# Spectral filter and gated MLP on one core: fifteen pairs of block products, denser dealing, low parts by GpSimd's queue, three twiddle copies

## The chip, the cores and the metric

One core of a Trainium2 chip runs the whole kernel. The metric is device time in microseconds (us). Before the change three runs took 1389.22, 1392.01 and 1394.37 us; the median is 1392.01. PE is the matrix engine, DVE the vector engine, ACT the scalar engine, POOL is GpSimd, SP the engine that here only issues DMAs. A DMA is issued by SP or by GpSimd, each in the order of its own instructions.

## The reference

```python
def reference(A_x, A_w_r, A_w_i, B_x, B_w_gate, B_w_up, B_w_down, gate_w):
    x = A_x                                            # 1 x 2048 x 576
    g = sigmoid((x * gate_w).sum(-1, keepdims=True))
    X = rfft2(x, axes=(-2, -1)) * (A_w_r + 1j * A_w_i)
    a = irfft2(X, s=(2048, 576), axes=(-2, -1))        # spectral branch
    h = gelu(B_x @ B_w_gate) * (B_x @ B_w_up)          # 576 -> 4608
    b = h @ B_w_down                                   # 4608 -> 576
    return g * a + (1 - g) * b
```

In this kernel the MLP reads the same x. All is float32.

## The kernel before

**The MLP is PE's work.** A float32 operand is split into a high part (rounded for the fast matmul) and a low part (the rest); a product takes three matmuls: high by high, low by high, high by low. The 4608 hidden features are 36 weight blocks of 128, taken in 18 pairs. Tokens are taken in two halves of 1024 (p = 0, 1), each as two column blocks of 512 (tb = 0, 1). One step n of the main loop is one pair of weight blocks for one tb: four chains (line 756, `chain`) of 14 matmuls of 512 columns, gate and up for each of two weight blocks, and, for the step before, four `down` (line 836) that multiply by the down weights (48 matmuls of 288 columns). Results go to a staging tile `stg` (four buffers) and from there into `yd` in DRAM, by a DMA on GpSimd's queue that adds to what is there; the first of each is a plain store on SP.

**Products.** For p = 1 the last pairs are done otherwise (`products`, line 1023): the two column blocks of tokens and two parts of the features form a 2 by 2 block product, done as seven products of sums (Strassen's way, in Winograd's form), each seven matmuls for gate and for up (`seven`, line 1009), with the sums of weights made by DVE (`prep_b`, line 985) and the sums of outputs added up by DVE (line 1051). That is 98 matmuls of 512 columns for a pair, where the ordinary way takes 112. The pairs from `FIRST` on go this way: i = 4 to 17 before. The operands are sums of x that are made once (`operands`, `last_operand`).

**Low parts in DRAM.** Weight blocks are needed twice, for p = 0 and p = 1. The low part of a weight block is a subtraction by DVE. For the first 2 x `FIRST` weight blocks, which p = 1 takes the ordinary way, `lower` (line 730) stores the low part in DRAM (`lo`) when p = 0 makes it, and p = 1 loads it instead of making it: 640 KB for the gate and up weights (into `gu`, three buffers) and 288 KB for the down weights (into `dn`, four buffers). Before, these loads are issued by SP, among the loads of raw weights (`raws<-wgu`, `raws<-wd`) and of x for the second half (`xraw<-xt`, line 1177, through four small buffers that ACT and DVE empty).

**The spectral branch runs beside it, mostly on DVE and ACT.** It is a generator that yields its costs: row transforms of the two halves (`forward_rows`), a column stage (`columns`) with its own matmuls on PE (line 274), and the way back (`last_tiles`, `inverse_rows` for h = 0 and 1). The matmuls of the MLP earn credit, `RATE` us for each us of PE time (`tick`, line 645); the MLP's own DVE work is taken from the credit. At each `gap` (line 653; twelve in a step n) the generator is run while there is credit, and stops early where it yields None. So `RATE` sets how much DVE work is queued per us of PE time, and so in which step each part of the branch stands. In the column stage a second generator (`beside`, line 293) does work on other tiles with what credit is left. `at(n, fn)` puts an instruction n gaps later. The results of the branch are added to `yd` by GpSimd: from `til` for h = 0 (line 607), from `xraw` and `cns` for h = 1 (line 597).

**Twiddles** multiply a complex tile by a constant rotation: ACT makes a scaled copy, DVE combines it with the tile (`_twiddles`, line 104 on). Whole tiles are turned by `tile_twiddles` (line 414), with two temporary tiles in the column stage and four in `last_tiles`.

**Operands** of the products are made in `operands`, woven into the last inverse transform by `woven` (line 562): at each second step of the main generator before.

Of the kernel before, what the change touches and what calls it, by code (L numbers as in the profile page):

```python
# [26 lines left out]
SW = 2 * (KF + 1)  # L27
ROWS = 5120
UNIT = ROWS // 4
RATE = 1.04  # L30
STEP = 6
FIRST = 4
ROW_BLOCK = (0, 6, 3, 5, 8, 1, 2, 7, 4)


# [68 lines left out]
def _twiddles(eng, act, unit, real, imag, places, tmps, sgn, cost):  # L104

    todo = list(places)
    ahead = min(2, len(tmps) - 1)

    def scaled(i):
        if i < len(todo):  # L110
            at, n = todo[i]
            s = 1.0 if n == 4 else sgn * math.sin(math.pi * n / 8)
            act.activation(tmps[i % len(tmps)][0], unit(*at), AF.Copy, scale=s)

    yield None
    for i in range(ahead):
        scaled(i)
    yield None
    for i, (at, n) in enumerate(todo):
        scaled(i + ahead)  # L120
        c, (_, tr, ti) = math.cos(math.pi * n / 8), tmps[i % len(tmps)]
        xr, xi = real(*at), imag(*at)
        if n == 4:
            act.activation(xr, ti, AF.Copy, scale=-float(sgn))
            act.activation(xi, tr, AF.Copy, scale=float(sgn))
            continue
        eng.scalar_tensor_tensor(xr, xr, c, ti, op0=ALU.mult, op1=ALU.subtract)
        yield cost
        eng.scalar_tensor_tensor(xi, xi, c, tr, op0=ALU.mult, op1=ALU.add)
        yield cost  # L130


def _block_of_token():
# [25 lines left out]
def _build(nc, tc, a):  # L159
    with ExitStack() as ctx:  # L160
# [8 lines left out]
        def f(x):  # L169
            return x.bitcast(F32)  # L170
# [59 lines left out]
        def columns():  # L230
# [62 lines left out]
            def beside():  # L293

                more = gates()
                tmps = [flat[:, SW * i:SW * (i + 1)] for i in (1, 2)]
                for d in range(1, 4):
                    yield from tile_twiddles(d, TAKEN, -1, tmps)
                    yield from four(d, TAKEN, sp, -1)
                    made[0] = d  # L300
                for d in range(3):
                    while gone[0] < (4 * d + 5) * STEP + 5:
                        yield next(more, None)
                    yield from four(d, range(4), sp, 1)
                yield from more
                for k in (1, 2):
                    yield from tile_twiddles(k, LEFT, 1, tmps)
# [19 lines left out]
            for kb in range(18):  # L327
# [18 lines left out]
                for g in range(STEP):  # L346
                    if g == 0:
                        while kb % 4 == 2 and kb < 14 and made[0] < kb // 4 + 1:
                            credit[0] -= next(side[0])
                        if on:  # L350
                            v = product(0, kb, xh, xl)
                            load_ww(kb + 1)
# [60 lines left out]

        def tile_twiddles(k, at, sgn, tmps):

            tmps = [(x, x[:, 0:NK], x[:, NK:]) for x in tmps]
            places = [((k, at[o]), o * k) for o in range(1, 4)]
            yield from _twiddles(vec, act, lambda d, e: T[:, d, e], lambda d, e: T[:, d, e, re],
                                 lambda d, e: T[:, d, e, im], places, tmps, sgn, 0.5)

        def last_tiles():

            rows = rows_tile()
            sp = rows[:, 0:4 * SW].rearrange("p (e k) -> p e k", e=4)
            yield from tile_twiddles(3, LEFT, 1, [rows[:, SW * i:SW * (i + 1)] for i in range(4, 8)])
            yield None
            yield from _butterfly(vec, lambda i: T[:, i], lambda i: T[:, i, :, re], lambda i: T[:, i, :, im],
                                  range(4), sp, 1, (2.6, 1.35))
# [132 lines left out]

        def woven(main, other):

            n, free = 0, 0
            for v in main:
                yield v
                n += 1
                if n % 2 == 0 and reloaded[0] and count[0] > free:
                    w = next(other, 0.0)
                    if w is None:  # L570
                        free = count[0]
# [158 lines left out]
        def lower(key, g, r, cost):  # L730
            j, i = key[1], key[0] == "dn"
            if NT <= j < NT + 2 * FIRST:
                nc.sync.dma_start(f(g[:, 1]), lows[j - NT][i])
                return

            def run():
# [574 lines left out]
```

## Time and profile before

| what | value |
|---|---|
| median of three runs | 1392.01 us |
| the profiled execution | 1387.69 us |
| its span (first to last instruction) | 1385.8 us |
| mean granted PE clock | 0.998 |
| matmuls | 7490 |

The page of the profile gives busy time by engine, and the span in 40 slices of 34.6 us. A digit is the busy share in tenths, 9 standing for 90% and more:

```profile
PE   9999999999999999999998999999999999999998
DVE  6989999998877876999979873587777777777776
ACT  5553434355656665444464549445555555555552
POOL 0021111121222211111141023212111121111110
DMA  9577765668899996556789588767667667776776
```

The stages lie so in time: p = 0 with the row transforms to about 320 us, the column stage to about 540, the way back to about 820; p = 1 begins in slice 21, and products run from 884 us to the end. A matmul's shown end is modelled and overlaps the next, so PE reads as busy through short waits; where it loses time is seen better from the windows and from the list of waits, where the engine that waited stands first and what released it second.

### The profile page before, as it was taken

What the parts mean: (1) busy time and instruction counts of PE and PEld (TensorE: products, weight loads), DVE (VectorE), ACT (ScalarE), POOL (GpSimd) and SP (SyncE); (2) the same over time, 40 slices, a digit from 0 to 9 for tenths busy, and PEclk for the clock granted to TensorE, in tenths of its full rate; (3) what the DMA queues carried; (4) which work ended last, traced back from release to release, by engine and by line L of the source; (5) the groups of instructions that cost most, each with busy time, mean ns of one, the idle gap of its engine ahead of it and who ended that gap; (6) DMA issues with size and microseconds to landing.
All of it is one profiled execution on the core that took longest, in us unless ns stands there. A gap on an engine that the chain in (4) does not pass through costs nothing.

```text
span 1385.8 us, 20125 instructions
## 1 busy us (share of the span) xinstructions
PE 1366.2 (99%) x7490; PEld 1206.0 (87%) x7490; DVE 1119.8 (81%) x1649; ACT 703.8 (51%) x1095; POOL 266.2 (19%) x326
## 2 busy tenths in 40 slices
PE   9999999999999999999998999999999999999998
PEld 7888888888888888888887888888888888888887
DVE  6989999998877876999979873587777777777776
ACT  5553434355656665444464549445555555555552
POOL 0021111121222211111141023212111121111110
PEclk9999999999999999999999999999999999999999
DMA  9577765668899996556789588767667667776776
GB/s 341 198 179 153 180 116 97 123 117 185 213 272 260 247 235 121 99 112 124 148 185 253 197 171 189 141 128 131 130 129 130 130 130 131 127 129 130 131 154 172
DMA packets 102226, 226.65 MB, mean 164 GB/s; under 512 B 12400, under 2 KB 22640, under 8 KB 101744
## 3 DMA queue, kind: packets, MB, share of 16 engines
q0 software_dynamic: 45248, 92.56, 44.0%
q1 hardware_dynamic: 56880, 132.81, 30.2%
q8 instruction: 59, 0.97, 0.3%
q14 instruction: 39, 0.32, 0.1%
HBM read 118.56 MB, written 99.61 MB: 157 GB/s over the span
## 4 chain that ended last, share of the span: by engine, by line
PE 58%; DMA 1%; DVE 1%; ACT 0%; issue 0%; SPq 0%; DVEq 0%; ACTq 0%
PE pdn L821 20%; PE pgu L1016 4%; PE pgu L1018 4%; PE pgu L1017 4%; PE px L1016 3%; PE px L1018 3%; PE px L1017 3%; PE pgu L762 2%; PE pgu L763 2%; PE pgu L761 2%; PE px L761 2%; PE px L763 2%; PE px L762 2%; PE pgu L1019 2%; PE px L1019 1%; DMA gu<-lo 1%
## 5 line engine op out<-in xcount | busy, mean ns | idle before, releaser
L834 POOL DMA_DIRECT2D yd<-stg x264 | 230.1, 872 | 1028.3 <-ACT stg L846 975.3
L846 ACT ACTIVATE stg<-pdn,omg 128x576 f32<-128x576 f32 x272 | 201.9, 742 | 380.2 <-PE pdn L821 282.1
L821 PEld LDWEIGHTS pdn<-dn,hb 128*128 128x128 f32 x2760 | 382.0, 188 | 11.6 <-DVE raws L875 0.5
L821 PE MATMUL pdn<-dn,hb 128*128 128x288 f32 x2760 | 389.9, 295 | 0.2 <-DVE raws L875 0.2
L762 PE MATMUL pgu<-xhi,gu 128*128 128x512 f32 x440 | 172.5, 392 | 4.2 <-DMA gu<-lo 3.9
L761 PE MATMUL pgu<-xhi,gu 128*128 128x512 f32 x440 | 172.6, 392 | 1.1 <-ACT gl L799 1.1
L763 PE MATMUL pgu<-xlo,gu 128*128 128x512 f32 x440 | 172.1, 391 | 0.0
L213 ACT ACTIVATE gu<-raws 128x1280 fp32r<-128x1280 f32 (+3 forms) x84 | 86.4, 1029 | 38.8 <-PE px L767 28.3
L762 PEld LDWEIGHTS pgu<-xhi,gu 128*128 128x128 f32 x440 | 82.9, 189 | 19.7 <-DMA gu<-lo 4.4
L761 PE MATMUL px<-xhi,gu 128*128 128x512 f32 x256 | 100.0, 390 | 0.0
L763 PE MATMUL px<-xlo,gu 128*128 128x512 f32 x256 | 99.8, 390 | 0.0
L762 PE MATMUL px<-xhi,gu 128*128 128x512 f32 x256 | 99.7, 389 | 0.0
L763 PEld LDWEIGHTS pgu<-xlo,gu 128*128 128x128 f32 x440 | 83.0, 189 | 18.1
L761 PEld LDWEIGHTS pgu<-xhi,gu 128*128 128x128 f32 x440 | 83.0, 189 | 16.3 <-ACT gl L799 1.5
L821 PEld LDWEIGHTS pdn<-dn,gu 128*128 128x128 f32 x672 | 92.2, 188 | 2.1
L821 PE MATMUL pdn<-dn,gu 128*128 128x288 f32 x672 | 93.5, 295 | 0.0
L807 DVE TENSOR_TENSOR hb<-gl,hb 128x512 fp32r<-128x512 f32 x88 | 60.4, 687 | 38.0 <-ACT hb L213 37.9
L799 ACT ACTIVATE gl<-pgu 128x512 f32<-128x512 f32 x55 | 32.8, 596 | 92.3 <-PE pgu L768 85.8
L1034 DVE TENSOR_TENSOR xraw<-xraw 128x512 f32<-128x512 f32 x56 | 38.8, 693 | 31.2 <-ACT xraw L1042 30.7
L1051 DVE TENSOR_TENSOR gl<-gl,pgu 128x512 f32<-128x512 f32 x56 | 38.3, 684 | 27.8 <-PE pgu L1019 27.8
L763 PEld LDWEIGHTS px<-xlo,gu 128*128 128x128 f32 x256 | 48.1, 188 | 10.4
L213 ACT ACTIVATE hb<-gl 128x512 fp32r<-128x512 f32 x88 | 54.9, 624 | 3.3 <-DVE gl L803 3.3
(220 smaller groups left out, 2659.7 us busy)
## 6 DMA issues: line engine op xcount, KB each, us to landing
yd<-stg POOLq DMA_DIRECT2D x264, 288.0 KB, 5.1
raws<-wgu SPq DMA_DIRECT2D x42, 640.0 KB, 5.5
raws<-wd SPq DMA_DIRECT2D x72, 288.0 KB, 3.1
quads<-ws SPq DMA_DIRECT2D x24, 384.0 KB, 4.5
colm<-col POOLq DMA_DIRECT2D x32, 256.0 KB, 6.3
raws<-ws SPq DMA_DIRECT2D x21, 384.0 KB, 4.3
lo<-gu SPq DMA_DIRECT2D x8, 640.0 KB, 4.5
gu<-lo SPq DMA_DIRECT2D x8, 640.0 KB, 6.1
```

What stands on the lines that cost most here:

```text
L213: act.activation(o, i, AF.Copy)
L761: pe.matmul(ps, w[:, 0, k, c], xhi[tb][:, k], start=k == 0, stop=False)
L762: pe.matmul(ps, w[:, 1, k, c], xhi[tb][:, k], start=False, stop=False)
L763: pe.matmul(ps, w[:, 0, k, c], xlo[tb][:, k], start=False, stop=False)
L807: vec.tensor_tensor(h[:, 1], g, f(h[:, 0]), ALU.subtract)
L821: pe.matmul(ps[half], h[:, l, c], d[:, q, half * HD:(half + 1) * HD], start=part == 0 and n == 0, stop=part == 1 and n == 2)
L834: pl.dma_start(yd[u], o, accum_op=ALU.add)
L846: put(u, lambda o: act.activation(o.rearrange("p (c k) -> p c k", c=2), v[:, :, 0:HD], AF.Copy, scale=omg[:, u:u + 1]), i == 0)
L1016: pe.matmul(ps, hi[:, c], xh[:, t], start=t == 0, stop=False)
L1017: pe.matmul(ps, lo[:, c], xh[:, t], start=False, stop=False)
L1018: pe.matmul(ps, hi[:, c], xl[:, t], start=False, stop=False)
L1019: pe.matmul(ps, w[:, 512 + P * s:512 + P * (s + 1)], xt, start=False, stop=True)
```

## The change

There are four parts. `FIRST` goes from 4 to 3: pairs 3 to 17 are done by products, fifteen instead of fourteen, and low parts of six instead of eight weight blocks are stored and loaded. `RATE` goes from 1.04 to 1.08, and `woven` takes an item of the operands after every step of the main generator instead of every second. The loads of low parts are issued by GpSimd instead of SP. `tile_twiddles` uses a new `_three_twiddles`: all three scaled copies are made at once, into three temporary tiles, and two gaps pass before DVE uses them.

```diff
-RATE = 1.04
+RATE = 1.08
 STEP = 6
-FIRST = 4
+FIRST = 3
...
+def _three_twiddles(eng, act, units, powers, tmps, sgn, cost):
+
+    yield None
+    for (x, _, _), n, (t, _, _) in zip(units, powers, tmps):
+        act.activation(t, x, AF.Copy, scale=1.0 if n == 4 else sgn * math.sin(math.pi * n / 8))
+    yield None
+    yield None
+    for (_, xr, xi), n, (_, tr, ti) in zip(units, powers, tmps):
+        c = math.cos(math.pi * n / 8)
+        for o, t, op, s in ((xr, ti, ALU.subtract, -float(sgn)), (xi, tr, ALU.add, float(sgn))):
+            if n == 4:
+                act.activation(o, t, AF.Copy, scale=s)
+            else:
+                eng.scalar_tensor_tensor(o, o, c, t, op0=ALU.mult, op1=op)
+                yield cost
...
-                tmps = [flat[:, SW * i:SW * (i + 1)] for i in (1, 2)]
+                tmps = [flat[:, SW * i:SW * (i + 1)] for i in (1, 2)] + [tmp[:, 3 * SW:4 * SW]]
...
-                            credit[0] -= next(side[0])
+                            credit[0] -= next(side[0]) or 0.0
...
-            yield from _twiddles(vec, act, lambda d, e: T[:, d, e], lambda d, e: T[:, d, e, re],
-                                 lambda d, e: T[:, d, e, im], places, tmps, sgn, 0.5)
+            parts = [(x, x[:, 0:NK], x[:, NK:]) for x in tmps]
+            units = [(T[:, k, at[o]], T[:, k, at[o], re], T[:, k, at[o], im]) for o in range(1, 4)]
+            yield from _three_twiddles(vec, act, units, [o * k for o in range(1, 4)], parts, sgn, 0.5)
...
-            yield from tile_twiddles(3, LEFT, 1, [rows[:, SW * i:SW * (i + 1)] for i in range(4, 8)])
+            yield from tile_twiddles(3, LEFT, 1, [rows[:, SW * i:SW * (i + 1)] for i in range(4, 7)])
...
-            n, free = 0, 0
+            free = 0
             for v in main:
                 yield v
-                n += 1
-                if n % 2 == 0 and reloaded[0] and count[0] > free:
+                if reloaded[0] and count[0] > free:
...
-                nc.sync.dma_start(f(g[:, 1]), lows[j - NT][i])
+                pl.dma_start(f(g[:, 1]), lows[j - NT][i])
```

**The order on the DMA queues, at the end of p = 0.** On SP before, the load of the second weight block's low part (`gu_71`, from `lo_1280_115`) stands among loads of x and of raw weights:

```order
L733 DMA dn_73<-lo_576_114 128x576
L1177 DMA xraw<-xt 128x512 x2
L711 DMA raws<-wgu 128x1280
L712 DMA raws<-wd 128x576
L1177 DMA xraw<-xt 128x512 x2
L733 DMA gu_71<-lo_1280_115 128x1280
L1177 DMA xraw<-xt 128x512
L733 DMA dn_74<-lo_576_116 128x576
```

On GpSimd before, the same stretch: the adds of the spectral rows of h = 0 (from `til`), with the last adds of a step (`yd_103`, `yd_104`) and the first of the next (`yd_97`):

```order
L607 DMA yd_97<-til 128x576
L834 DMA yd_103<-stg_86 128x576
L607 DMA yd_98<-til 128x576
L834 DMA yd_104<-stg_87 128x576
L607 DMA yd_99<-til 128x576
L607 DMA yd_100<-til 128x576
L607 DMA yd_101<-til 128x576
L607 DMA yd_102<-til 128x576
L607 DMA yd_103<-til 128x576
L607 DMA yd_104<-til 128x576
L834 DMA yd_97<-stg_84 128x576
```

On GpSimd after the change, up to the same `yd_97` (lines are 15 to 17 further down in the new file):

```order
L622 DMA yd_101<-til 128x576
L622 DMA yd_102<-til 128x576
L849 DMA yd_101<-stg_84 128x576
L622 DMA yd_103<-til 128x576
L849 DMA yd_102<-stg_85 128x576
L622 DMA yd_104<-til 128x576
L849 DMA yd_103<-stg_86 128x576
L849 DMA yd_104<-stg_87 128x576
L748 DMA dn_73<-lo_576_114 128x576
L748 DMA gu_71<-lo_1280_115 128x1280
L849 DMA yd_97<-stg_84 128x576
```

The low parts moved from SP to GpSimd, between two steps' adds; the adds from `til` moved forward, ahead of the last two adds of the step.

**The order on ACT, at the first twiddles of the column stage.** Before, ACT's rows there (copies into `xraw` are the twiddles' scaled copies, lines 124 and 125 the turn by a quarter):

```order
L213 ACTIVATE colm<-til 128x580
L113 ACTIVATE xraw<-til 128x580 x3
L124 ACTIVATE til<-xraw 128x290
L125 ACTIVATE til<-xraw 128x290
L799 ACTIVATE gl_81<-pgu 128x512
```

After it, the rows of the same twiddles:

```order
L230 ACTIVATE gu_70<-raws 128x1280
L137 ACTIVATE xraw<-til 128x580 x2
L137 ACTIVATE tmp<-til 128x580
L814 ACTIVATE gl_82<-pgu 128x512
L861 ACTIVATE stg_84<-pdn,omg 128x576
L230 ACTIVATE hb_80<-gl_81 128x512
L861 ACTIVATE stg_85<-pdn,omg 128x576
L230 ACTIVATE til<-px_2708 128x290
L230 ACTIVATE colm<-til 128x580
L144 ACTIVATE til<-xraw 128x290 x2
```

The third copy goes into a tile of its own, and six instructions of the MLP and the column transform now stand between the copies and their first use on ACT, where before the use followed the copies at once.

**The order on PE, where the fifteenth pair begins.** Before, the last ordinary step of the pair that changes ends the previous pair's `down` and goes on with a chain of 14:

```order
L821 MATMUL pdn<-dn_73,hb_80 128x288 x6
L821 MATMUL pdn<-dn_74,hb_78 128x288 x6
L761 MATMUL px_7305<-xhi_63,gu_70 128x512
L762 MATMUL px_7305<-xhi_63,gu_70 128x512
L763 MATMUL px_7305<-xlo_65,gu_70 128x512
L761 MATMUL px_7305<-xhi_63,gu_70 128x512
```

After it, at the same place, the first product (seven matmuls for gate, then seven for up):

```order
L836 MATMUL pdn<-dn_73,hb_80 128x288 x6
L836 MATMUL pdn<-dn_74,hb_78 128x288 x6
L1031 MATMUL pgu<-xhi_63,gu_70 128x512
L1032 MATMUL pgu<-xhi_63,gu_70 128x512
L1033 MATMUL pgu<-xlo_65,gu_70 128x512
L1031 MATMUL pgu<-xhi_63,gu_70 128x512
```

All the matmuls behind this place move forward by one pair's difference. Those ahead of it are the same as before, but the column stage's stand a little earlier among them.

More of the change, by code (lines that the diff above doesn't have):

```diff
@@ L414, in tile_twiddles @@
         def tile_twiddles(k, at, sgn, tmps):
-            tmps = [(x, x[:, 0:NK], x[:, NK:]) for x in tmps]
-            places = [((k, at[o]), o * k) for o in range(1, 4)]
-            yield from _twiddles(vec, act, lambda d, e: T[:, d, e], lambda d, e: T[:, d, e, re],
-                                 lambda d, e: T[:, d, e, im], places, tmps, sgn, 0.5)
+            parts = [(x, x[:, 0:NK], x[:, NK:]) for x in tmps]
+            units = [(T[:, k, at[o]], T[:, k, at[o], re], T[:, k, at[o], im]) for o in range(1, 4)]
+            yield from _three_twiddles(vec, act, units, [o * k for o in range(1, 4)], parts, sgn, 0.5)
         def last_tiles():
```

## The prediction

> **What bounds the kernel now.** I read the page's first, second and fourth parts, then who waited for whom on PE, then the windows around PE's gaps, then the chain and SP's and GpSimd's timelines there.
>
> ```profile
> span 1385.8 us, 20125 instructions
> PE 1366.2 (99%) x7490; PEld 1206.0 (87%) x7490; DVE 1119.8 (81%) x1649; ACT 703.8 (51%) x1095; POOL 266.2 (19%) x326
> ```
>
> PE is busy 1366.2 of 1385.8 us: only less PE work, or fewer of the 19.6 us in which PE stands, can help. Where PE waits:
>
> ```profile
> PE px L274 <- DVE colm L267: 4.0, 2, 2.3
> PE pgu L762 <- DMA gu<-lo: 3.9, 1, 3.9
> PE px L274 <- issue: 1.5, 2, 0.9
> ```
>
> (Columns: total us, times, longest.) Line 274 is the column transform of the spectral branch, line 762 the second matmul of a chain, the one that reads a weight block's low part. The windows show what each place loses (PE, PEld, DVE, ACT, POOL busy; clock; DMA share; GB/s):
>
> ```profile
> 320.00:540.00 220.00, 212.18 (x1190) 187.30 (x1189) 172.77 (x297) 134.78 (x227) 49.84 (x67) 1.00 0.93 223
> 731.50:735.80 4.30, 0.37 (x3) 0.04 (x1) 4.20 (x7) 1.38 (x3) 0.00 (x0) 0.97 1.07 286
> 735.80:739.20 3.40, 3.40 (x9) 2.68 (x10) 0.65 (x2) 1.31 (x2) 0.00 (x0) 0.54 1.05 369
> ```
>
> Column stage: 220 - 212.18 = **7.8 us** idle. At 731.5: 4.30 - 0.37 = 3.9 us idle, and then 3.4 us at a granted clock of 0.54, which loses 3.4 x 0.46 = 1.6 us more although PE reads as busy. Together **5.5 us** for one wait. The rest of the idle time is start and end, which the change doesn't touch.
>
> **Part 1: the fifteenth pair.** Pair i = 3 of the second half of the tokens goes from two blocks of 4 ordinary chains a weight block to seven products. The chain of waits gives both periods:
>
> ```profile
> 658.35 3.18 PE pdn L821 x24
> 677.46 3.18 PE pdn L821 x24
> ...
> 985.73 3.18 PE pdn L821 x24
> 1020.78 3.18 PE pdn L821 x24
> ```
>
> An ordinary block (half a pair) takes 677.46 - 658.35 = 19.11 us, a pair 38.22; a pair of products takes 1020.78 - 985.73 = 35.05. Nothing in either waits, so the edit is worth **-3.17 us** (14 fewer 512-column matmuls). The additions and splits that it moves to DVE and ACT lie in product pairs where DVE has room (81% over the span).
>
> **Part 2: low parts by GpSimd's queue.** What delayed the load that PE waited for, on SP's timeline and then on the chain:
>
> ```profile
> 712.42 2.34 SPq L1177 DMA_DIRECT2D xraw<-xt  x2
> 714.81 1.21 SPq L711 DMA_DIRECT2D raws<-wgu  x1
> 716.07 0.93 SPq L712 DMA_DIRECT2D raws<-wd  x1
> 717.09 0.99 SPq L1177 DMA_DIRECT2D xraw<-xt  x2
> 718.17 0.51 SPq L733 DMA_DIRECT2D gu<-lo  x1
> ...
> 718.17 17.54 DMA gu<-lo
> 735.76 0.79 PE pgu L762
> ```
>
> SP issues in order, so the low part stood behind four loads of xraw, which themselves wait until the earlier xraw has been read, and then took 17.54 us to land. GpSimd meanwhile issued its adds into yd:
>
> ```profile
> 706.91 0.87 POOL L834 DMA_DIRECT2D yd<-stg  x1 [1.90 <-ACT stg L846]
> 707.45 1.22 POOL L607 DMA_DIRECT2D yd<-til  x1
> 707.99 1.57 POOL L834 DMA_DIRECT2D yd<-stg  x1
> 708.54 4.60 POOL L607 DMA_DIRECT2D yd<-til  x4
> ...
> 716.90 0.87 POOL L607 DMA_DIRECT2D yd<-til  x1 [1.79 <-DMA yd<-stg]
> 721.83 0.87 POOL L834 DMA_DIRECT2D yd<-stg  x1 [4.07 <-ACT stg L846]
> ```
>
> and what a load takes by either queue (KB, median us to landing):
>
> ```profile
> quads<-ws SPq DMA_DIRECT2D x24, 384.0 KB, 4.5
> gu<-lo SPq DMA_DIRECT2D x8, 640.0 KB, 6.1
> quads<-ws POOLq DMA_DIRECT2D x4, 384.0 KB, 7.1
> yd<-til POOLq DMA_DIRECT2D x8, 288.0 KB, 12.5
> ```
>
> In the new order the low part follows the low part of dn_73 and stands ahead of the next block's yd<-stg, whose counterpart was issued at 721.83, and all eight adds from til come before the yd<-stg of yd_103 and yd_104, behind which six of them stood. Those two were issued at 707 and 708 us. So the low part is issued at some 709 to 721 us of this clock, and the adds that it competed with are issued before 707. By the same load on both queues GpSimd's costs 7.1 / 4.5 = 1.6 times as long: 6.1 x 1.6 = 9.8 us, so it lands by 719 to 731. PE asked at 731.5. At the old 17.54 us it would be late again by up to 721 + 17.5 - 731.5 = 7 us. The ends are 0 and -5.5 us; I take **-5.5**, since the xraw loads and the adds, the two things that made it late, are both gone from its way.
>
> What is queued behind it: on GpSimd a low part waits until PE has left the gu buffer, and the yd<-stg behind it wait with it, then ACT for one of four stg buffers. The order puts it at the end of the chain that frees the buffer, and GpSimd is 19% busy; 12 issues of 0.87 us are hidden there. SP loses the 16 loads (12 are left, on GpSimd) and four stores of low parts; its xraw, weight and operand loads no longer wait behind a gu buffer.
>
> The rule that speaks against this part concerns GpSimd's own issue; here are its issues (min/median/max ns):
>
> ```profile
> L834 POOL DMA_DIRECT2D yd<-stg x264: 847/866/1572, 70.3 to 1366.1; - x132
> L607 POOL DMA_DIRECT2D yd<-til x8: 866/1572/2978, 703.8 to 716.9; - x8
> ```
>
> The Trainium skill, "DMA: Bandwidth & Descriptors", section "SWDGE vs HWDGE vs iDMA", says that GpSimd writes its descriptors into SBUF, which VectorE locks it out of while it runs in its two-port mode, and that transfers of SP and ACT are immune. By that rule a load could be held as long as VectorE runs without a pause, and the wait would stay: -3.2 us in all instead of -8.7. The trace doesn't bear it out: 264 issues have a median of 866 ns, and none is over 1.6 us though DVE is busy 79.30 of 80 us in one stretch (below); only the burst of 703.8 to 716.9 is stretched.
>
> **Part 3: denser dealing (1.08 for 1.04), operands at every step.** In each us of PE time 1.08 / 1.04 = 3.85% more DVE work is queued. Whether DVE can take it:
>
> ```profile
> 40.00:320.00 280.00, 280.00 (x1523) 247.17 (x1522) 264.30 (x346) 127.80 (x198) 49.17 (x60) 1.00 0.67 145
> 560.00:820.00 260.00, 256.07 (x1390) 225.88 (x1389) 241.16 (x306) 120.94 (x188) 46.71 (x55) 0.99 0.71 164
> 560.00:640.00 80.00, 80.00 (x436) 70.62 (x435) 79.30 (x77) 32.75 (x48) 14.44 (x17) 1.00 0.59 111
> ```
>
> DVE is idle 280 - 264.3 = 15.7 us in the first row stage and 260 - 241.2 = 18.8 in the second; 3.85% of them is 10.8 and 10.0. So it fits over a stage, but not over 560 to 640, with 0.7 us idle for 3.1 us of added work. There the queue of DVE grows, and the cover is this:
>
> ```profile
> 634.16 0.68 DVE L807 TENSOR_TENSOR hb<-gl,hb 128x512 fp32r<-128x512 f32 x1
> 639.24 3.18 PE pdn L821 x24
> ```
>
> The low half of hb is ready at 634.84, and the matmuls that need it come after 639.24: DVE may be 4.4 us later before PE stands. 3.1 us fit. I take **0**; if the cover is gone, each us of lag costs one.
>
> **Part 4: three copies, two gaps ahead.** It removes DVE's waits of this kind in whole-tile twiddles:
>
> ```profile
> DVE til L127 <- ACT xraw L113: 9.7, 6, 3.6
> ```
>
> 9.7 us of DVE idle time, none of it PE's; the instructions are the same. It shortens DVE's queue in the column stage, where the denser side work lengthens it by 3.85% of 172.77 = 6.7 us. These nearly cancel, so the 7.8 us of PE waits there stay: **0**, bounded by -4 (half of them gone) and +5 (PE stands for what of the 6.7 us meets the chain).
>
> **Sum.** 1385.8 - 3.2 - 5.5 = 1377.1 us of span. The profiled execution took 1387.69, 1.9 outside its span; the median of the runs is 1392.01, 4.3 above it. I subtract the same 8.7 from the median: **1383.3**, rounded to 1383.5.
>
> **Rivals.**
>
> *The low part is late all the same* (0.15): behind adds on GpSimd's queue, or held as by the skill's rule. Only part 1 is left: 1388.8. For it: 12.5 us to landing for adds from til; against: the order, and 10 us of room.
>
> *The column stage gets worse* (0.13). Its products wait on DVE's low part (4.0 us above); with more side work ahead of it the 7.8 us become about 13: 1388.5. *It gets better* (0.10) if the copies' 9.7 us weigh more: 1379.5.
>
> *The fifteenth pair starts too early* (0.07), so that the saving isn't had. Before, the spectral branch's last adds and the first product stood so:
>
> ```profile
> L597 POOL DMA_DIRECT2D yd<-cns x4: 866/1014/1217, 850.1 to 867.6; - x4
> ...
> 883.78 0.24 PE pgu L1016
> ```
>
> 16 us apart. The products move 38.2 us forward, the branch by at most 3.7% (1 - 1.04/1.08) of the 867.6 - 220 us outside the column stage, 24 us: the two nearly meet. In the order the last operand stands ahead of the last adds, so I expect no wait; if ACT and DVE are late, PE loses up to 5 us: 1388.5.
>
> *DVE becomes the bound* (0.09). If windows at 99% mean that DVE takes no more, PE waits for the 3.85% there. Over both stages that is (280 + 260) x 3.85% = 20.8 us; with the cover of 4.4 us taken off in each, 12.0: 1395 to 1404, slower than before. It decides once the lag passes that cover. For it: 79.30 of 80. Against: the idle time of both stages exceeds the added work.
>
> **Numbers.** The forecast has 0.46. 0.5% is 7.0 us, about what a measurement of this kernel can tell from no change: 1385.0 and 1399.0. Of the forecast's own spread (2.5 us either way) 0.38 is below 1385.0; with the better column stage, faster 0.48. Slower is 0.07 of the DVE rival; the rest, 0.45, is no change. The range runs from the better column stage with a little more, 1378.5, to the late low part with a slightly worse one, 1391.5; outside are the DVE rival and tails.
>
> **What would show it.** PE 14 matmuls fewer; no wait of line 762's counterpart on gu<-lo and a clock of 1.00 between 700 and 760 us; idle PE of 4 to 13 us in the column stage; no PE wait on DVE's hb in the row stages; first product near 840 us (883.8 - 38.2 - 5.5), without idle PE ahead of it. I am wrong if the low parts land later than 20 us after issue, or if PE idles at 100 to 300 or 540 to 680 us.

## The result and the profile after

| what | before | after |
|---|---|---|
| median in the same comparison (5 runs each) | 1390.34 us | 1376.05 us |
| lowest and highest | 1389.22, 1394.37 | 1375.33, 1376.27 |
| the profiled execution | 1387.69 us | 1376.05 us |
| its span | 1385.8 us | 1374.1 us |

The ratio is 0.9895 with a 95% interval of 0.9877 to 0.9913: about 1% faster, and 2.45 us below the low end of the predicted range. The sign was right; the forecast gain of 8.7 us was too small. The profiled pair differs by 11.6 us, the medians by 14.3.

The head of the page after, then who PE waited for (total us, times, longest), then the windows around the places the prediction named (idle PE is the window's length less PE's busy time):

```profile
span 1374.1 us, 20146 instructions
PE 1362.7 (99%) x7476; PEld 1204.1 (88%) x7476; DVE 1138.7 (83%) x1683; ACT 708.0 (52%) x1102; POOL 273.1 (20%) x338
```

```profile
PE pdn L836 <- ACT stg L861: 1.9, 1, 1.9
PE pgu L1150 <- DVE gate L1146: 1.5, 1, 1.5
PE px L795 <- DVE xhi L1156: 1.0, 1, 1.0
PE px L291 <- ACT dn L230: 0.9, 1, 0.9
PE px L1032 <- DVE gu L1018: 0.6, 1, 0.6
```

```profile
40.00:300.00 260.00, 260.00 (x1412) 229.43 (x1411) 251.38 (x328) 118.89 (x184) 44.69 (x55) 1.00 0.65 141
300.00:520.00 220.00, 218.43 (x1230) 193.71 (x1229) 182.04 (x313) 138.95 (x234) 50.71 (x68) 1.00 0.95 227
540.00:680.00 140.00, 140.00 (x767) 123.84 (x766) 133.65 (x158) 61.95 (x93) 26.78 (x31) 1.00 0.62 119
690.00:760.00 70.00, 70.00 (x389) 62.20 (x388) 67.76 (x89) 36.18 (x62) 17.82 (x24) 1.00 0.90 240
800.00:860.00 60.00, 57.49 (x307) 49.88 (x306) 33.05 (x53) 41.64 (x58) 18.92 (x23) 1.00 0.77 158
```

PE has 14 matmuls fewer. The wait on the low part is gone, and the clock is 1.00 between 690 and 760 us. The row stages have no idle PE. The column stage (300 to 520 now) idles 1.57 us where it idled 7.82. New is 2.51 us of idle time between 800 and 860.

For a full account I add up, over all matmuls, what the time from one start to the next has beyond its usual length (0.228 us for 512 columns, 0.137 for the shorter ones), in the traces of the two profiled executions; this takes in the slow clock after a wait. Called **lost time** below:

| place | before | after |
|---|---|---|
| first matmuls | 4.07 | 5.11 |
| column stage | 10.35 | 3.18 |
| low part, near 731 us | 5.64 | 0 |
| near 811 us and at the first product | 0 | 3.14 |
| end | 0.49 | 0.49 |
| sum | 20.6 | 11.9 |

The sums differ by 8.6 us; the pair's 3.2 on top make 11.8, which is the span's difference of 11.7. The first matmuls lose between 4.0 and 5.3 us in all the kernels below, whatever was edited, so that row says nothing of the change.

The 10.35 us before are of four kinds: 4.5 at two column products that wait for a low part, 3.3 at three that wait behind the filter step (shown below), 1.0 at one that waits for a copy by ACT, and 1.4 at an MLP chain that waits for ACT's `gl`; the rest is under 0.3.

### The profile page after: what moved, and what is told of

It is laid out like the page before. It is cut to its first block, busy times and chain, and to the rows that moved or that the text cites. A ratio compares the mean times of both kernels' runs of the same rounds, so it can differ in the third digit from the quotient of the medians.

```text
span 1374.1 us, 20146 instructions
## 1 busy us (share of the span) xinstructions
PE 1362.7 (99%) x7476; PEld 1204.1 (88%) x7476; DVE 1138.7 (83%) x1683; ACT 708.0 (52%) x1102; POOL 273.1 (20%) x338
## 4 chain that ended last, share of the span: by engine, by line
PE 92%; DVE 2%; issue 2%; DMA 2%; ACT 1%; POOL 0%; SPq 0%; DVEq 0%; POOLq 0%; ACTq 0%
PE pdn L836 31%; PE pgu L776 6%; PE pgu L777 6%; PE pgu L778 6%; PE pgu L1031 4%; PE pgu L1033 4%; PE pgu L1032 4%; PE px L776 4%; PE px L778 4%; PE px L777 4%; PE px L1032 3%; PE px L1031 3%; PE px L1033 3%; PE pgu L1034 2%; PE pgu L782 2%
## 5 line engine op out<-in xcount | busy, mean ns | idle before, releaser
L836 PEld LDWEIGHTS pdn<-dn,hb 128*128 128x128 f32 x2712 | 375.5, 188 | 13.8 <-ACT stg L861 2.3
L836 PE MATMUL pdn<-dn,hb 128*128 128x288 f32 x2712 | 383.5, 295 | 2.1 <-ACT stg L861 1.9
L776 PE MATMUL pgu<-xhi,gu 128*128 128x512 f32 x416 | 162.7, 391 | 0.0
L778 PE MATMUL pgu<-xlo,gu 128*128 128x512 f32 x416 | 162.3, 390 | 0.0
L777 PE MATMUL pgu<-xhi,gu 128*128 128x512 f32 x416 | 162.2, 390 | 0.0
L836 PEld LDWEIGHTS pdn<-dn,gu 128*128 128x128 f32 x720 | 98.8, 188 | 2.3
L836 PE MATMUL pdn<-dn,gu 128*128 128x288 f32 x720 | 100.2, 295 | 0.0
L776 PE MATMUL px<-xhi,gu 128*128 128x512 f32 x248 | 96.8, 390 | 0.0
L777 PE MATMUL px<-xhi,gu 128*128 128x512 f32 x248 | 96.6, 389 | 0.0
L778 PEld LDWEIGHTS pgu<-xlo,gu 128*128 128x128 f32 x416 | 78.1, 188 | 17.1
L777 PEld LDWEIGHTS pgu<-xhi,gu 128*128 128x128 f32 x416 | 78.1, 188 | 14.1 <-DVE gu L1165 0.4
L776 PEld LDWEIGHTS pgu<-xhi,gu 128*128 128x128 f32 x416 | 78.1, 188 | 14.0 <-ACT gl L814 0.3
L1066 DVE TENSOR_TENSOR xraw<-gl,px 128x512 f32<-128x512 f32 x60 | 41.3, 688 | 21.1 <-PE px L1034 20.4
```

The lines of the kernel that those rows point to most:

```text
L776: pe.matmul(ps, w[:, 0, k, c], xhi[tb][:, k], start=k == 0, stop=False)
L777: pe.matmul(ps, w[:, 1, k, c], xhi[tb][:, k], start=False, stop=False)
L778: pe.matmul(ps, w[:, 0, k, c], xlo[tb][:, k], start=False, stop=False)
L836: pe.matmul(ps[half], h[:, l, c], d[:, q, half * HD:(half + 1) * HD], start=part == 0 and n == 0, stop=part == 1 and n == 2)
L1066: vec.tensor_tensor(o, x, v, ALU.add)
```

## The experiments

Sixteen kernels, four to twelve runs each. Spans and idle times are those of the profiled execution; column idle is idle PE in a window over the stage (320 to 540 us where the stage begins as before, 300 to 540 for b_three, 300 to 520 otherwise). The ratios compare with runs of the kernel before from the same session.

| kernel | median us (range) | ratio to before, 95% | span | column idle |
|---|---|---|---|---|
| the change | 1376.05 (1375.33–1376.27) | 0.9895 [0.9877, 0.9913] | 1374.1 | 1.57 |
| b_three | 1379.79 (1377.32–1383.04) | 0.9922 [0.9905, 0.9940] | 1381.2 | 2.24 |
| b_rate108 | 1376.04 (1374.39–1377.45) | 0.9895 [0.9879, 0.9911] | 1374.2 | 0.00 |
| b_three_rate | 1378.06 (1377.60–1379.88) | 0.9912 [0.9896, 0.9928] | 1375.8 | 1.56 |
| b_lows_pool | 1387.97 (1384.12–1390.82) | 0.9977 [0.9965, 0.9988] | 1389.0 | 9.00 |
| a_old_twiddles | 1374.14 (1371.93–1377.11) | 0.9874 [0.9855, 0.9892] | 1370.2 | 0.00 |
| a_lows_sp | 1375.80 (1375.00–1376.36) | 0.9884 [0.9869, 0.9899] | 1374.2 | 1.57 |
| a_first4 | 1377.95 (1377.45–1379.08) | 0.9906 [0.9887, 0.9925] | 1376.1 | 1.57 |
| b_108_cols | 1381.32 (1380.71–1381.73) | 0.9925 [0.9912, 0.9937] | 1378.9 | 4.79 |
| b_108_rows | 1379.71 (1379.18–1380.91) | 0.9914 [0.9899, 0.9929] | 1379.1 | 2.35 |
| b_low_early | 1389.23 (1384.81–1391.38) | 0.9977 [0.9964, 0.9990] | 1383.5 | 5.69 |
| a_low_early | 1376.94 (1376.26–1377.62) | 0.9896 [0.9874, 0.9917] | 1375.5 | 2.71 |
| a_old_low_early | 1373.35 (1372.95–1374.10) | 0.9873 [0.9851, 0.9894] | 1370.9 | 0.03 |
| b_hold01 | 1378.99 (1377.60–1380.31) | 0.9917 [0.9903, 0.9932] | 1376.8 | 4.24 |
| a_hold01 | 1376.46 (1374.02–1377.65) | 0.9896 [0.9880, 0.9911] | 1374.8 | 1.66 |
| a_old_hold01 | 1372.40 (1369.51–1374.78) | 0.9868 [0.9848, 0.9888] | 1368.3 | 0.28 |
| a_old_both | 1370.61 (1370.06–1374.72) | 0.9862 [0.9845, 0.9880] | 1368.3 | 0.67 |

Names that begin with b_ are the kernel before with an edit, those with a_ the changed kernel with one.

### One part at a time, on the kernel before

**b_three**: the three copies alone (the function, the third temporary tile, the callers).

```diff
-                tmps = [flat[:, SW * i:SW * (i + 1)] for i in (1, 2)]
+                tmps = [flat[:, SW * i:SW * (i + 1)] for i in (1, 2)] + [tmp[:, 3 * SW:4 * SW]]
...
+            yield from _three_twiddles(vec, act, units, [o * k for o in range(1, 4)], parts, sgn, 0.5)
```

> Before, with the three copies alone. Theory 'copies' (the 6 us that the column stage saved come from ACT making all scaled copies early, so that DVE does not stand for them and the column products get their low parts in time): idle PE of 320 to 540 us falls from 7.8 to under 3 us, the time by about 5 us, to 1385. Theory 'dealing' (they come from the side work being queued earlier): the column stage keeps 6 to 9 us and the time stays within 2 us of before. Theory 'place' (what PE waits for there depends on where the products fall among the steps of the MLP, and any shift redraws it): idle anywhere from 2 to 10 us. In all three the wait for gu<-lo near 731 us stays (3 to 6 us with its slow clock).

**b_rate108**: the denser dealing alone.

```diff
-RATE = 1.04
+RATE = 1.08
...
-                if n % 2 == 0 and reloaded[0] and count[0] > free:
+                if reloaded[0] and count[0] > free:
```

> Before, with RATE 1.08 and the operands at every step alone. Theory 'copies': column stage idle 7 to 10 us, as before or worse. Theory 'dealing': under 4 us. Theory 'place': 2 to 10 us. The adds from til move forward by some 14 us while low parts stay with SP. If the adds made the low part late, the wait for gu<-lo is gone or under 2 us (time about 1385); if SP's own order made it late, it stays at 3 us or more. If DVE cannot take the denser dealing, PE waits for hb or gl in the row stages, 5 us or more in all.

**b_three_rate**: both.

> Before, with three copies and denser dealing, low parts on SP, fourteen pairs. Theory 'copies': column stage idle under 3 us, like b_three. 'dealing': under 4, like b_rate108. If both are needed it is under 3 here and over 5 in each alone. The time is that of the changed kernel plus 3.2 us (the fifteenth pair) plus whatever the low part still waits (0 to 5.5 us): 1379 to 1385.

**b_lows_pool**: the low parts by GpSimd alone.

```diff
-                nc.sync.dma_start(f(g[:, 1]), lows[j - NT][i])
+                pl.dma_start(f(g[:, 1]), lows[j - NT][i])
```

> Before, with the low parts loaded by GpSimd's queue alone. If SP's order made the low part late: the wait for gu<-lo and the slow clock behind it are gone, 5.5 us less, 1385, and the spread of the runs falls from 5 us to about 1. If the adds from til made it late (they still stand ahead of it, now on its own queue): the wait stays at 3 us or more, 1390. The column stage keeps its 7.8 us in both.

Windows of b_rate108, then of b_three, then of b_lows_pool, over the column stage and the place of the low part:

```profile
300.00:520.00 220.00, 220.00 (x1246) 196.61 (x1245) 181.59 (x313) 140.47 (x235) 51.97 (x70) 1.00 0.95 229
690.00:760.00 70.00, 69.94 (x378) 61.34 (x377) 67.14 (x90) 35.81 (x61) 11.63 (x14) 1.00 0.87 228
```

```profile
300.00:540.00 240.00, 237.76 (x1335) 212.04 (x1333) 194.06 (x328) 146.37 (x244) 55.80 (x76) 0.99 0.95 224
690.00:760.00 70.00, 65.71 (x348) 57.44 (x347) 60.24 (x72) 35.83 (x53) 17.95 (x21) 0.95 0.85 210
```

```profile
320.00:540.00 220.00, 211.00 (x1173) 186.97 (x1172) 171.27 (x293) 130.07 (x219) 48.99 (x67) 0.98 0.91 217
690.00:760.00 70.00, 69.80 (x377) 61.07 (x376) 59.33 (x77) 38.19 (x56) 24.07 (x31) 1.00 0.91 218
```

The dealing alone gives the whole change's time, 1376.04, where I had expected about 1385. It takes the column stage's idle time to 0, though DVE does more work there (181.59 us in 220 against 172.77 before), and the wait on the low part with it: the adds from `til` are issued at 676.7 to 689.0 us instead of 703.8 to 716.9, and the load lands in 8.8 us instead of 17.5. The copies alone take the waits of the column products as well (0.1 us of lost time left there; the 2.24 us idle is a chain that waits for ACT's `gl`), and leave the low part's wait; b_three is 5 us faster than I expected. The queue alone takes the low part's wait, and nothing in the column stage; its profiled execution is the longest of its twelve runs, which spread over 6.7 us, not the 1 us that I expected without that wait. Copies on top of the dealing are worse than the dealing alone.

### One part undone, on the changed kernel

**a_old_twiddles**: the old twiddles again (the reverse of b_three).

> The changed kernel with the old twiddles (two temporary tiles, no two gaps ahead); pair, dealing and GpSimd's low parts stay. Theory 'copies cost on top of the dealing': they put the column stage's products at other gaps, where 3.2 us of waits stand that the dealing alone does not have (0.2); so this kernel loses under 1 us there and is about 2 to 3 us faster than the changed one: 1373 to 1374.5. Theory 'the pair gives nothing' (1376.04 with 14 pairs and the dealing alone is already the whole change's time): 1376 +- 0.7, with a new wait near the first product as large as the pair's 3.2 us. Theory 'copies help beside the dealing too': slower than the changed kernel, 1378 or more.

**a_lows_sp**: low parts by SP again (the reverse of b_lows_pool).

> The changed kernel with the low parts loaded by SP as before. Theory 'queue is redundant beside the denser dealing' (the dealing alone already removed the wait on the low part): 1376 +- 0.7, no PE wait of line 778's counterpart on gu<-lo. Theory 'SP's order still makes it late': the wait of 4 to 5.5 us is back near 725 us and the time is 1380 to 1381.5.

**a_first4**: fourteen pairs again.

```diff
-FIRST = 3
+FIRST = 4
```

> The changed kernel with fourteen pairs of products instead of fifteen. Theory 'the pair gives 3.2 us less its new wait': the changed kernel saves 14 matmuls and loses 0.9 us before the first product, so this one is 2.0 to 2.5 us slower than it: 1378 to 1378.6, with no wait before the first product. Theory 'the pair gives nothing': 1376 +- 0.7. Theory 'the pair gives its whole 3.2 us': 1379.2.

Without the copies the column stage has no idle PE, and the median is 1.9 us lower, though two of the four runs (1377.11 and 1375.76) are in or above the range of the change: likely, by the ratios' overlapping intervals not certain. With SP's queue the time is the same, 1375.80: beside the denser dealing that edit does nothing. The fifteenth pair is worth 1377.95 - 1376.05 = 1.9 us, which is its 3.17 less about the 0.92 of lost time before the first product. By the trace of before it would cost more without the dealing: there the branch's last adds run to 867.6 us, and the first product would come near 845 (883.8 less the 38.2 of a pair). No run tried that.

### Where the dealing acts in the column stage

**b_108_cols** and **b_108_rows**: 1.08 only inside the column stage, or only outside it (`wide` is false inside). Both also take operands at every step, as b_rate108 does; the words "nothing else changed" below leave that out.

```diff
-            credit[0] += RATE * us
+            credit[0] += (1.04 if wide[0] else RATE) * us      # b_108_cols
+            credit[0] += (RATE if wide[0] else 1.04) * us      # b_108_rows
```

> The kernel before with the credit at 1.08 only inside the column stage and 1.04 elsewhere; nothing else changed. Theory 'dealing inside the stage': the stage's own chain gets credit at more gaps, so its low parts are not queued behind lumps of other work; PE loses under 3 us there instead of 10.4 (the low-part wait stays): 1381 to 1385. Theory 'place': the stage begins at the same gap as before, so waits like those of before (6 to 12 us) stay: 1388 to 1391.

> The kernel before with the credit at 1.08 everywhere but in the column stage, where it stays 1.04; the stage begins 10 gaps earlier, as with 1.08 throughout. Theory 'dealing inside the stage': PE loses 6 to 12 us there as before; the low-part wait goes (the adds come earlier), so 1383 to 1387. Theory 'place': under 3 us are lost there: 1375.5 to 1379. Rival on DVE in the row stages: no PE wait on hb there by either theory.

Both fall between the two theories: 6.5 us of lost time in the stage with the one, 4.9 with the other (1.3 of it at the column products, the rest at one chain that waits for ACT, with the slow clock behind it), 10.35 before. The wait on the low part falls to 1.9 us of lost time with the one and goes with the other. Neither the rate in the stage nor its beginning decides alone. So each stalled product is read by itself.

### Low parts of the stage a gap earlier

**b_low_early**, **a_low_early**, **a_old_low_early**: the two subtractions `low` of the column stage (line 267) are queued one gap earlier, in the kernel before, the changed one, and the changed one with the old twiddles.

```diff
+                        if was:
+                            low(yl, vs, yh)
                     elif g == 2:
                         if on:
                             filter_start()
-                        if was:
-                            low(yl, vs, yh)
+                        if kb + 1 < 16:
+                            low(xl2, two(Z[kb + 1]), xh2)
...
-                        if kb + 1 < 16:
-                            low(xl2, two(Z[kb + 1]), xh2)
```

> The kernel before with the two subtractions that make the low parts of the column stage's operands queued one gap (about 2 us) earlier; nothing else changed. Theory 'queue ahead' (a product waits because DVE, never idle, has other work queued ahead of its low part): the lows end up to 2 us sooner, the waits in the column stage fall from 10.4 us to under 4, the low-part wait near 731 stays: 1382 to 1386. Rival 'ACT' (the high-part copy on ACT is what is late): DVE now waits for that copy and the products wait as before: 1389 to 1393.

> The changed kernel with the same two subtractions one gap earlier. Theory 'queue ahead': the 3.2 us of waits in the column stage fall to under 1: 1373 to 1374.5. Rival 'ACT': no change, 1376 +- 0.7, or slower if the work behind the early subtractions is late for its own reader.

> The changed kernel with the old twiddles and with the two subtractions one gap earlier. Theory 'copies cost only by where they put the products': with the lows early it no longer matters which twiddles are used, so the same time as the changed kernel with early lows, within 1 us (1372.5 to 1374.5). Theory 'copies cost in themselves': 2 us faster than it, 1371 to 1372.

A miss for my theory: with the lows early, the stall at 533 us goes (2.6 us of lost time), but the others stay (5.69 us of idle time in place of 7.82; 2.71 in place of 1.57). Those behind the filter step are now whole at the product's first matmul, where before a part stood inside the product. The trace shows what that matmul waits for. DVE's and PE's timelines of the kernel before, at one of its stalls:

```profile
349.39 0.47 DVE L127 SCALAR_TENSOR_TENSOR til<-til,xraw 128x290 f32<-128x290 f32 x1 [1.88 <-ACT xraw L113]
349.77 0.46 DVE L129 SCALAR_TENSOR_TENSOR til<-til,xraw 128x290 f32<-128x290 f32 x1
351.94 0.46 DVE L127 SCALAR_TENSOR_TENSOR til<-til,xraw 128x290 f32<-128x290 f32 x1 [1.71 <-ACT xraw L113]
352.32 0.45 DVE L129 SCALAR_TENSOR_TENSOR til<-til,xraw 128x290 f32<-128x290 f32 x1
352.69 0.45 DVE L127 SCALAR_TENSOR_TENSOR til<-til,xraw 128x290 f32<-128x290 f32 x1
353.06 0.45 DVE L334 TENSOR_TENSOR til<-px,til 128x290 f32<-128x290 f32 x1
353.55 0.46 DVE L335 TENSOR_TENSOR til<-px,til 128x290 f32<-128x290 f32 x1
...
354.11 1.16 PE L274 MATMUL px<-colm 128*128 128x290 f32 x4 [0.61 <-issue]
```

Lines 334 and 335 (`filter_start`) read `px`, the result bank of the product before; the kernel has one bank of each of the two kinds (`ps_x`). The second read ends at 353.55 + 0.46 = 354.01, and the next product starts at 354.11. The reads stood on DVE behind five instructions of side work (a whole-tile twiddle, in whose middle DVE stood 1.71 us for ACT's scaled copy). The same holds for the changed kernel at its longest stall, on DVE and PE:

```profile
441.17 0.45 DVE L351 TENSOR_TENSOR til<-px,til 128x290 f32<-128x290 f32 x1
441.66 0.46 DVE L352 TENSOR_TENSOR til<-px,til 128x290 f32<-128x290 f32 x1
...
442.22 1.43 PE L291 MATMUL px<-colm 128*128 128x290 f32 x6 [0.88 <-ACT dn L230]
```

441.66 + 0.46 = 442.12, and 0.10 later PE starts. The profile names ACT's copy into `dn`, which ended at 441.80 and has nothing to do with this product: where an engine named had long been done, look for the reader of the buffer that PE is about to write. Of the nine stalls at column products in the two kernels, six end 0.06 to 0.10 us after a filter step does (354, 462 and 511 us before; 359, 442 and 490 after); the two longest of before (332 and 533, 4.5 us together) end 0.06 after a `low` does. The last one (502, 1.0 us) is the bank as well, but its reader is ACT, with the first of two copies out of `px`; ACT's and PE's timelines of the kernel before:

```profile
501.81 0.71 ACT L213 ACTIVATE til<-px 128x290 f32<-128x290 f32 x2
...
502.26 1.07 PE L274 MATMUL px<-colm 128*128 128x290 f32 x6 [0.72 <-ACT til L213]
```

The first copy ends at 502.21 and PE starts 0.05 later.

### No side work ahead of the filter step

**b_hold01**, **a_hold01**, **a_old_hold01**: side work isn't dealt in the two gaps ahead of the filter step; **a_old_both** has the lows a gap earlier as well.

```diff
+                    quiet[0] = g in (0, 1)
                     yield None
+                    quiet[0] = False
...
-                    while side and credit[0] > 0:
+                    while side and credit[0] > 0 and not quiet[0]:
```

> The kernel before, but no side work is dealt in the two gaps ahead of the filter step of the column stage. Theory 'bank' (a product waits for its one result bank, which VectorE's filter step frees, behind side work in VectorE's queue): the stalls that begin at the end of a filter step (354, 462, 511 us in the kernel before, 3.5 us) go; those on the low part (332 and 533, 4.5 us) may stay; with the low-part wait at 731 the time is 1385 to 1388.5. Rival 'the chain itself is late' (the filter waits for ACT's copy or for its inputs, not for side work): the stalls stay, 1390 to 1393.

> The changed kernel with no side work in the same two gaps. Theory 'bank': its three stalls (359, 442, 490 us; 3.2 us) begin at the end of a filter step and go: 1372.5 to 1374. Rival 'the chain itself is late': 1376 +- 0.7.

> The changed kernel with the old twiddles and with no side work in the same two gaps. Theory 'copies matter only by where they put VectorE's work': no stall over 0.5 us in the column stage with either twiddles, so the same time as the changed kernel with these gaps free, within 1 us: 1372.5 to 1374. Theory 'copies cost in themselves': 1 to 2 us faster than that kernel.

> The changed kernel with the old twiddles, no side work in the two gaps, and the low parts queued one gap earlier. Theory 'bank': nothing is left to gain in the column stage, the time is that of the kernel without the earlier low parts within 0.7 us, and its runs spread by under 2 us. Rival: the low parts still cost in some runs: 1 us faster and a smaller spread than without.

The same product as above, in b_hold01, on DVE and on PE:

```profile
350.41 0.46 DVE L334 TENSOR_TENSOR til<-px,til 128x290 f32<-128x290 f32 x1 [2.69 <-ACT til L213]
350.90 0.46 DVE L335 TENSOR_TENSOR til<-px,til 128x290 f32<-128x290 f32 x1
...
353.54 0.97 PE L274 MATMUL px<-colm 128*128 128x290 f32 x6
```

The bank is free at 351.36, 2.2 us before PE wants it. In the profiled executions of these four kernels no column product stalls over 0.2 us, save the one on the low part at 332 us in b_hold01 (1.94), which lies ahead of the gaps that the edit touches. The stalls behind the filter step that the kernel before and the change have are gone in b_hold01 and a_hold01, as the theory of the bank has it. The two with the old twiddles are no test of it: a_old_twiddles had lost only 0.1 us at the products. The edit moves side work to other gaps, so that a mere shift cleared these places is not excluded; against it speaks that b_108_cols, b_108_rows, b_lows_pool, b_low_early and a_low_early, where work is shifted too, keep stalls behind the filter step.

Not all of the time follows. b_hold01 is faster than I expected (1378.99 against 1385 to 1388.5): the stall at 533 went as well, and the wait at 731 fell to 1.5 us of lost time. What its column stage still loses, 5.3 us, is 1.9 at the product at 332 and 3.4 at three chains that wait for ACT's `gl`. a_hold01 is no faster than the change, because other waits came in. Its PE waits, and ACT's timeline at the first of them:

```profile
PE pdn L839 <- ACT stg L864: 3.6, 4, 1.8
PE pgu L779 <- ACT gl L817: 1.7, 1, 1.7
```

```profile
378.92 0.69 ACT L230 ACTIVATE colm<-til 128x580 fp32r<-128x580 f32 x1 [3.78 <-DMA til<-cns]
379.51 0.58 ACT L817 ACTIVATE gl<-pgu 128x512 f32<-128x512 f32 x1
```

ACT stood 3.78 us for a transfer of the column stage, and the MLP's `gl` stood behind it. With the old twiddles the second is absent and the first 0.5 us, and the time is 1372.40, or 1370.61 with the lows early: **faster than both kernels** (every run is below the fastest of the change, 1375.33), 0.9862 with 0.9845 to 0.9880. The 1.8 us between these two are not shown to be a difference: their runs cover each other (1369.51 to 1374.78 and 1370.06 to 1374.72), and both profiled executions took 1370.08. That a_old_both still spreads over 4.7 us, where I expected under 2, is not explained.

In three settings (unedited, low_early, hold01) the old twiddles are 1.9, 3.6 and 4.1 us faster than the new by the medians; only with low_early do the runs not overlap. I expected at most 1 us of difference in the last two. With low_early most of it is the products again (3.3 us of lost time there with the new twiddles, 0.2 with the old). With hold01 the products lose nothing either way, and the new twiddles lose 5.3 us near 710 to 740 us, mostly to ACT's `stg`; the old lose nothing there. Why the copies put ACT's work there stays open.

## Why the prediction was wrong

Parts 1 and 2 came out at their sizes. The step that failed is part 4: its 0 for the column stage measured 7.2 us of gain. Part 3's 0 missed 2.2 us the other way, and the anchor of the sum another 4.3.

**Part 1 (-3.17 us): right in size, less a wait.** The 14 matmuls are gone. The rival that the pair starts too early came true in small; DVE's and PE's timelines at the first product of the changed kernel:

```profile
839.97 0.96 DVE L1011 TENSOR_TENSOR cns<-misc,raws 128x768 f32<-128x768 f32 x1 [1.15 <-DMA yd<-cns]
840.85 0.68 DVE L1018 TENSOR_TENSOR gu<-raws,gu 128x512 fp32r<-128x512 f32 x1
...
841.59 0.50 PE L1032 MATMUL px<-xhi,gu 128*128 128x512 f32 x1 [0.64 <-DVE gu L1018]
```

A sum of weights needs `cns`, which the branch's last adds still read; DVE waits 1.15 us for them, PE loses 0.92. I had set up to 5 us for this rival, and predicted a start near 840 us: 840.55 in the trace.

**Part 2 (-5.5 us): right in size (5.6 us of lost time went), and its two reasons were one too many.** I said that the xraw loads and the adds "are both gone from its way". Either is enough, but they do different things. b_rate108 left the load on SP behind the xraw loads and took the adds out of its way: it landed in 8.8 us instead of 17.5, 6.0 us before PE could use it, and the wait went (69.94 of 70 us busy). b_lows_pool left seven of the eight adds ahead of the load: it still took 15.9 us, but was issued 17.0 us before PE could use it instead of 13.5, and landed 1.1 us in time (69.80). So the long landing goes with the adds, whichever queue carries the load, and beside the denser dealing the queue adds nothing (a_lows_sp). The low parts' issues and landings after the change (min/median/max ns of an issue; KB and median us to landing), then the landings by SP in a_lows_sp:

```profile
L748 POOL DMA_DIRECT2D gu<-lo x6: 540/720/892, 688.5 to 783.1; - x6
gu<-lo POOLq DMA_DIRECT2D x6, 640.0 KB, 7.3
gu<-lo SPq DMA_DIRECT2D x6, 640.0 KB, 7.1
```

The load that PE had waited for was issued at 709.93 us and landed in 10.2 us, where I had worked out 9.8; that was near by luck, since its working took a load by GpSimd to cost 1.6 times one by SP, and the medians here are 7.3 and 7.1 us.

The Trainium skill, "DMA: Bandwidth & Descriptors", section "SWDGE vs HWDGE vs iDMA", says that VectorE's two-port mode locks GpSimd out of the SBUF state that it writes its descriptors to. No sign of it is in this trace: no issue of a low part is over 0.9 us, with DVE busy 67.76 of 70 us around it; in which mode DVE ran, the trace doesn't say.

**Part 3 (0): right for the row stages, wrong for one other place.** PE is busy 260.00 of 260 and 140.00 of 140 us there, with DVE busy 251.38 of 260 us in the first, 96.7%, where it was 264.30 of 280, 94.4%: the cover of `hb` was enough. DVE as the bound is ruled out. But at 811 us there is a wait I had not named (1.9 us, 2.2 lost). ACT's timeline of the changed kernel:

```profile
805.82 3.84 ACT L230 ACTIVATE sx<-xraw 32x512 fp32r<-32x512 f32 x6 [0.77 <-DVE sx L911]
809.70 1.39 ACT L611 ACTIVATE xraw<-rows,gs 128x576 f32<-128x576 f32 x1
...
812.50 0.74 ACT L861 ACTIVATE stg<-pdn,omg 128x576 f32<-128x576 f32 x1
```

Six copies of operand tails and a scaling of rows stand on ACT, 5.3 us without a pause, then three shorter instructions, and the `stg` that frees PE's bank stands behind them. b_rate108 has this wait too (1.9 us), before has none. Yet before has the same stretch on ACT:

```profile
839.87 3.82 ACT L213 ACTIVATE sx<-xraw 32x512 fp32r<-32x512 f32 x6
843.73 1.44 ACT L596 ACTIVATE xraw<-rows,gs 128x576 f32<-128x576 f32 x1
```

PE loses nothing there, nor near it in b_108_cols, which takes operands at every step too. No kernel with 1.04 outside the column stage waits near 811, and all with 1.08 do (0.4 to 2.3 us at the first matmul behind it). So it is not more work on ACT, nor the operands' pace alone; the denser dealing put this stretch ahead of a `stg` that PE soon needed. I had costed the operands only where DVE has room, and left ACT out.

**Part 4, the column stage (0): this step failed.** "These nearly cancel, so the 7.8 us of PE waits there stay" added up DVE work: 6.7 us more of it against 9.7 us of waits removed. The amount was not what PE waited for. DVE's busy time in 220 us rose from 172.77 to 182.04 us and the idle PE fell from 7.82 to 1.57. What counts is which side work stands on DVE just ahead of the filter step that frees the product's bank, and of the low parts. b_hold01 shows this for 6.8 of the 10.35 us: the same rate, the same start, no side work in two gaps, and the three stalls at the filter step (3.3 us), the one at the low part at 533 (2.6) and the one at 502 (1.0) are gone. The denser dealing and the copies each happen to clear the products (0.1 us or less of lost time at them); together they leave 2.9. That they clear them is measured; why their order suits and the two together less so was not worked out. The rival "it gets better" had the sign, with 0.10, and about half of the size: -4 for lost time that fell from 10.35 to 3.18; its reason, the weight of the copies, is not the whole of it: the copies alone take the products' waits, and so does the dealing alone. I also read 7.8 us from the windows where starts show 10.35, since a matmul's modelled end covers part of a wait; the bound of "half of them gone" was no bound.

**The anchor.** I subtracted the profile's 8.7 us from the median, which stood 4.3 above the profiled execution. That surplus was most likely made of waits that went, too. 54 runs of the kernel before, from four sessions, by the granted clock that each had:

| granted clock | runs | mean us |
|---|---|---|
| 0.994, 0.995 | 5 | 1393.96 |
| 0.996 | 17 | 1392.83 |
| 0.997 | 18 | 1391.03 |
| 0.998 | 13 | 1389.14 |
| 0.999 | 1 | 1387.67 |

The profiled execution before, at 1387.69, was one of the shortest. The 54 runs spread over 8.5 us, the five of the change over 0.9, and its profiled execution is its median. In the trace of before a wait of 3.9 us was followed by 3.4 us at a clock of 0.54; b_three, whose wait there is 4.3, has 6.8 us of slow clock behind it. One such stretch of 3.4 us at half clock takes 0.0012 off the mean clock of the span, so by estimate the runs at 0.995 had two or three more than those at 0.998. b_lows_pool, which differs from before in the queue alone, was profiled in such a run (1390.82 us at 0.995; its shortest took 1384.12 at 1.000): its column stage loses 16.6 us, with three stretches of 3.4 us at half clock behind waits that lost 2.3 to 3.6. That the long runs of before come from the same is argued, not shown: no profile of one was taken. Of the 7.45 us between 1383.5 and 1376.05, 3.0 are the span (1377.1 expected, 1374.1 found: 7.2 gained in the column stage, 3.1 lost near 811 and 840 and 1.0 at the start) and 4.3 the surplus of the median; the rest is rounding.

## What to carry to other kernels

When PE waits for an in-order engine, don't weigh how much work is added to that engine, but list what stands on it directly ahead of the instruction that PE waits for, and of the reader that frees PE's next result bank. The engine that did not cause the wait may be the one that the profile names: where it ended well before the wait did (0.4 us above), look for a reader of the bank that ended 0.1 us before. Where the runs of a kernel spread by several us, the one profiled execution can be far from the median (4.3 us here), and a gain worked out from it should not simply be taken off the median. The spread doesn't measure the waits: b_108_cols loses 13.7 us in its trace and its six runs spread over 1.0, a_old_hold01 loses 6.2 and its four spread over 5.3.

## What was unexpected of the hardware

The granted clock fell after waits of very different length: 3.9 us in the kernel before brought one stretch of 3.4 us at half speed, 4.3 us in b_three 6.8 us, and 1.9 us at 807 in b_rate108 3.4 us, while the 1.9 us at 811 in the change brought none (1.00 from 800 to 860). a_low_early waits 1.87 us for the same `stg` at the same place as the change (PE goes on at 813.23 and 813.29), and has 3.4 us at half speed behind it. The windows of b_rate108, then of a_low_early:

```profile
800.00:860.00 60.00, 58.15 (x308) 51.01 (x308) 12.20 (x19) 36.22 (x49) 17.49 (x20) 0.97 0.79 162
800.00:860.00 60.00, 57.96 (x302) 50.53 (x302) 32.12 (x51) 41.42 (x58) 18.41 (x23) 0.97 0.77 154
```

So a wait of 1.9 us costs about 2 or 3.5 us; what decides it isn't shown here.
